# Moving one set of small matmuls ahead of another in a fused attention and MLP kernel

## The chip, the cores and the metric

The kernel runs on one core of a Trainium2 chip. The metric is the device time of one execution in microseconds. Three runs of the kernel before gave 688.54, 688.73 and 689.0 us, a median of 688.73 us. Beside these there is one profiled execution, with its own time and its own trace; all durations below come from it.

The core's engines work side by side, each through its own queue: TensorE does matmuls (PE in the profile; its weight loads are PEld), VectorE (DVE) and ScalarE (ACT) do the elementwise work, and SyncE (SP) issues the transfers. An instruction that needs another engine's result waits for it on a semaphore.

## The reference

There are 8 batches of 8 heads, 512 tokens, 32 state rows and a head width of 64. For each batch and head, the tokens read the state and the state reads the tokens, both through a softmax:

```
xread = softmax(scale * x @ state^T) @ state      # 512 rows a head
sread = softmax(scale * state @ x^T) @ x          # 32 rows a head
attn  = concat([xread, sread])                    # 544 rows a batch
h     = attn_as_4352_by_512 @ w_in                # w_in: 512 x 2048
out   = (h * sigmoid(1.702 h)) @ w_out            # w_out: 2048 x 512
```

The weights come as float64 values. The kernel reads them as pairs of 32-bit words and makes float32 values of them on the chip.

## The kernel before, in words

**Weights.** Each weight matrix is brought in as 16 pieces, the 16 of `w_in` first. A piece of `w_out` is a transfer of 512 KB into a buffer named `later` (`load_weight`, line 199), and then a series of steps called a round. On VectorE: a mask of the exponent bits (line 221), the fraction (239), the sign (245) and two products (258 and 264). On ScalarE, between the mask and the sign: two Relu instructions (lines 232 and 233, in `round_a`) that clamp the exponent to the range of float32. This document calls the pair the clamp. `powers_to` and `round_to` issue these steps ahead of need, so one call of `round_to` finishes one piece and starts the clamp of the next.

**The state, multiplied early.** The kernel doesn't compute `xread @ w_in` as it stands. `att_M(b, c)` (line 575) multiplies the state of batch b by column block c of `w_in` and keeps the product in a tile M; `up_x` (line 671) then multiplies M by the transposed attention weights (`aT`) in one step. `att_M` issues 16 small matmuls (64 rows by 32 columns of the array, line 430) into two PSUM banks, and two ScalarE copies (line 573) bring these into M. With its third argument set, the two banks are the pair with the tag `h`, which `up_x` also uses.

**The state's own read.** `att_sread(b)` (line 618) issues 64 small matmuls (128 by 32, line 629) and two ScalarE copies (line 635). For batch 1 it reads `eT`, which two VectorE transposes (line 605, `eT_turn`) make from a tile that has come back from HBM. `att_srT` (line 638) transposes the result on TensorE.

**Where the change lies.** The order of the work is that of the Python text: nothing is planned by costs, each engine takes its instructions in the order written. From line 1562 a loop over 8 block pairs computes batch 0's `gelu(h) @ w_out` by one step of Strassen's method: seven products P1 to P7 a pair, each of four matmuls (`pair`, line 1548), with sums of blocks made on VectorE by `pair_sums` and `left_sums` (line 1479). In between it completes `h` of batch 1 with `up_x`. The first pass (i = 0, lines 1568 to 1589) also holds the attention work that was left over: `att_sread(0)`, `att_M(1, 2)`, the transposes of `eT`, a `round_to`, `att_sread(1)` and `att_M(1, 3, True)`. After it, from line 1665 on, each batch goes through `strassen_two`, where a product has a second level of Strassen's method (lines 809 and 858) and the next batch's attention is hung into named places.

At line 1574 only one piece, number 19, is left for `round_to(nin + 4, 1)` to finish, and what it issues on ScalarE is the clamp of piece 20, whose mask (line 221) waits for that piece's transfer. Line 1583 is `up_x(1, 8)`. Its output takes the next bank of the pair `h`, which is the first of the two that `att_M(1, 3, True)` has just filled, so it can't begin before the first of that call's copies.

Of the kernel before, what the change touches and what calls it, by code (L numbers as in the profile page):

```python
# [20 lines left out]
def kernel(  # L21
# [72 lines left out]
    def att_ps(shape, name):  # L94
        return psA.tile(shape, FP32, tag="att", name=name)
# [151 lines left out]
    def round_b(i, ahead, follows, fill=None):  # L247


        if i not in begun:  # L250
            fraction(i)
        if i not in signed:
            sign(i)
        dst, sc = begun.pop(i), signed.pop(i)
        lo, _ = words(i)
        powers_to(ahead)

        nc.vector.scalar_tensor_tensor(dst, lo, 2.0**-32, dst.bitcast(I32), ALU.mult, ALU.add)
        del raw[i]
        if fill is not None:  # L260
            fill()
        elif follows and i + 1 in raw:
            fraction(i + 1)
        nc.vector.scalar_tensor_tensor(dst, dst, 2.0**-20, sc.bitcast(FP32), ALU.mult, ALU.mult)
# [13 lines left out]
    def powers_to(n):  # L278
        while done["a"] < min(n, len(PIECES)):
            load_weights(done["a"] + 1)  # L280
            round_a(done["a"])
            done["a"] += 1

    def refill():
        while done["b"] > NPR and done["load"] < len(PIECES) and before(done["load"]) < done["b"]:
            load_weights(done["load"] + 1)

    def round_to(n, ahead=AHEAD):

        nin = NFC * NPR  # L290
        while done["b"] < min(n, len(PIECES)):
            i = done["b"]
            powers_to(i + 1)
            round_b(i, min(i + 1 + ahead, i + 3 if i > nin + 3 else i + 2 if i >= nin else nin), i >= nin or i + 1 < nin and (i + 1 < n or i >= NPR))
            done["b"] += 1
            refill()
# [128 lines left out]
    def by_state(b, ps, rhs):  # L425

        for j in range(NPR):
            for g in range(NG):
                rows, st = slice(D * g, D * (g + 1)), slice(Ns * j, Ns * (j + 1))
                nc.tensor.matmul(ps[g][st], state_of(b, NG * j + g, g), rhs(rows, j), start=True, stop=True)  # L430
# [140 lines left out]
    def M_copies(b, c):  # L571
        for g, ps in enumerate(M_banks.pop((b, c))):
            nc.scalar.copy(A[b]["M", c][:, g], ps)  # L573

    def att_M(b, c, spare=False, banks=None, copied=True):

        m = mpool.tile([P, NG, FC], FP32, tag=f"M{turns['M'] % NFC if b < 2 else c}", name=f"M_{b}_{c}")
        turns["M"] += 1
        A[b]["M", c] = m
        name = f"M_{b}_{c}_"  # L580
        ps = banks or [
            psH.tile([P, FC], FP32, tag="h", name=name + str(g)) if spare else att_ps([P, FC], name + str(g)) for g in range(NG)
        ]
        by_state(b, ps, lambda rows, j: w_in[c][rows, j])
        M_banks[b, c] = ps
        if copied:
            M_copies(b, c)
# [15 lines left out]
    def eT_turn(b, g):  # L603
        t = A[b]["eT"][:, g].rearrange("p c q -> p (c q)")
        nc.vector.transpose(t, t)
# [12 lines left out]
    def att_sread(b):  # L618

        a = A[b]  # L620
        ps = att_ps([P, NG, D], f"sr_{b}")
        for g in range(NG):
            for c in range(SCH):
                for j in range(NPR):
                    st = slice(Ns * j, Ns * (j + 1))
                    e, v = a["eT"][:, g, c, st], xn[b][:, NG * j + g, c]
                    if b:
                        e = a["eT"][:, g, j, Ns * c : Ns * (c + 1)]
                    nc.tensor.matmul(
                        ps[st, g], e, v,  # L630
                        start=(c == 0), stop=(c == SCH - 1),
                    )
        sr = apool.tile([P, P], FP32, tag="sr", name=f"sr_{b}", bufs=2)
        for g in range(NG):
            nc.scalar.activation(out=sr[:, D * g : D * (g + 1)], in_=ps[:, g], func=AF.Copy, scale=a["e2"][g][1])
        A[b]["sr"] = sr
# [11 lines left out]
    def gelus(n):  # L648
        for _ in range(n):
            fn, kw = waiting.pop(0)  # L650
            fn(**kw)
# [19 lines left out]
    def up_x(b, f, spare=False, bank=None, wait=False, dst=None):  # L671
        c, o = divmod(P * f, FC)
        m = A[b]["M", c]
        up(b, f, S, [m[:, g, o : o + P] for g in range(NG)], [A[b]["aT"][:, g] for g in range(NG)], spare, bank, wait, dst)
# [796 lines left out]
    def pieces(t, *shape):  # L1471
        n, k = shape
        return t.rearrange("p a b -> p (a b)").rearrange("p (n k t) -> p n k t", n=n, k=k)
# [7 lines left out]
    def four(t):  # L1481
        return t.rearrange("p a b -> p (a b)").rearrange("p (n t) -> p n t", t=HS)
# [15 lines left out]
    def turns_of(*lists):  # L1498

        for step in zip(*lists):  # L1500
            for fn, args in step:
                fn(*args)
# [4 lines left out]
    def left_sums(i):  # L1507

        u = ORDER[i] // 2
        (a11, a21), (a12, a22) = quarters(0, u, S), quarters(0, HF // 2 + u, S)  # L1510
        s1, s2, *s4 = (v[:, i % 4 : i % 4 + 2] for v in s_rooms)
        return [(tt, v) for v in ((s1, a21, a22, ALU.add), (s2, s1, a11), (a21, a11, a21), *((s, a12, s2) for s in s4))]
# [18 lines left out]
    def pair(i, *names):  # L1531

        f = ORDER[i]
        a11, a12, a21, a22 = a_of(f)
        s1, s2, s4 = s_of(i) if i >= 0 and names[0] not in ("P1", "P2") else (None,) * 3
        t = t24(i) if s1 is not None else None
        for name in names:
            lhs, rhs = {
                "P1": lambda: (a11, B11[:, f]),
                "P2": lambda: (a12, B21[:, f]),  # L1540
                "P5": lambda: (s1, T1[:, f]),
                "P6": lambda: (s2, t[:, 0]),
                "P7": lambda: (a21, B12[:, f]),
                "P3": lambda: (s4, B22[:, f]),
                "P4": lambda: (a22, t[:, 1]),
            }[name]()
            for r in range(2):
                nc.tensor.matmul(  # L1548
                    ps7[name][:, HN * r : HN * (r + 1)], lhs[:, P * r : P * (r + 1)], rhs,
                    start=(i == 0 and r == 0), stop=(i == HF - 1), skip_group_check=True,  # L1550
                )
# [10 lines left out]
    for i in range(HF):  # L1562
        round_to(nin + 2 * i + 2)
        gelus(len(waiting))
        if i == 3:
            nc.scalar.copy(G[1, f_early // 2][:, f_early % 2], early)
        if i == 0:
            pair(i, "P1")
            att_sread(0)
            att_M(1, 2, banks=bank_o[1::2])  # L1570
            turns_of(left_sums(0))
            for g in range(NG):
                eT_turn(1, g)
            round_to(nin + 4, 1)
            att_sread(1)
            att_M(1, 3, True)
            t_room.append(pieces(apool.tile([P, NG, SCH * P], FP32, tag="eT", name="t_room_1"), 2, 2))
            s_rooms.append(four(apool.tile([P, NG, NB * Ns], FP32, tag="e1", name="s4_room")))
            pair_sums(i, left_sums(0)[3:])
            pair(i, "P2")  # L1580
            f_early = rest.pop(0)
            early = xn[0].rearrange("p h c d -> p (h c d)")[:, :S]
            up_x(1, f_early, dst=early)
            att_srT(0)
            att_srT(1)
            powers_to(nin + 6)
            pair(i, "P6")
            ps7["P7"], ps7["P3"] = (psH.tile([P, FC], FP32, tag="h", name=f"down_{k}") for k in (7, 3))
            ps7["P4"], up_bank = (att_ps([P, FC], f"down_{k}") for k in (4, "up"))
        else:  # L1590
            pair_sums(i)
            pair(i, "P1", "P2")
        if i == 2:
            G[1, f_early // 2] = free.pop(0)
        if i > 1 and i % 2 == 0:
            up_x(1, rest.pop(0), bank=up_bank, wait=True)
        if i == HF - 1:
            k1 = s_rooms[0][:, :2]
            nc.scalar.copy(k1, ps7["P1"].rearrange("p (r n) -> p r n", r=2))
        late()  # L1600
        if i > 1 and i % 2:
            up_x(1, rest.pop(0), bank=up_bank if i < HF - 1 else bank_o[0], wait=True)
        if i == HF // 2 + 1:
            load_state(2)
            load_x_squares(2)
# [140 lines left out]
```

## Time and profile before

| what | value |
|---|---|
| median of three runs | 688.73 us |
| the profiled execution's own time | 689.52 us |
| its span, first to last instruction | 687.7 us |
| TensorE busy (matmuls) | 677.1 us, 98% |
| VectorE busy | 558.6 us, 81% |
| ScalarE busy | 327.4 us, 48% |
| mean granted TensorE clock | 0.998 |

The span and the profiled time differ by 1.8 us, which lie around the instructions. A difference in the span is taken as a difference in the time. In the answers below, a line of the timeline reads: start in us from the span's beginning, length in us, engine, source line, operation, what it writes and reads, tile of the array for matmuls, elements, count; a last bracket gives idle time of that engine before it, and what ended it. The line is often that of a helper. A matmul's end is modelled, and the next one normally starts before it, so the distance between two starts says better than a length what a group costs in a full stream.

### The profile page before, as it was taken

The page shows a single profiled execution, that of the slowest core. Times are in us where ns is not written, and L with a number is a line of the kernel's source. Part 1 is how long each engine was busy: PE and PEld are TensorE (multiplying, and loading weights), DVE is VectorE, ACT ScalarE, POOL GpSimd, SP SyncE. Part 2 cuts the span into 40 slices and gives each one's busy share as a digit, 9 for nine tenths or more (in the row PEclk, how much of TensorE's full clock was granted, in tenths as well). Part 3 has the DMA queues.
Part 4 walks back from the last instruction along what each step waited for, and adds up shares of the span by engine and source line. Part 5 has one row for each costly group of instructions (what it writes and reads, how often), then busy time and mean ns, then how long its engine had stood idle before and what let it go on. Part 6 is the DMA issues. An engine that isn't in the chain of part 4 may idle for free.

```text
span 687.7 us, 13606 instructions
## 1 busy us (share of the span) xinstructions
PE 677.1 (98%) x5347; PEld 577.8 (84%) x5347; DVE 558.6 (81%) x1066; ACT 327.4 (48%) x725; POOL 1.5 (0%) x10
## 2 busy tenths in 40 slices
PE   8999999999999999999999999999999999999996
PEld 4443587769989899889988998989988998999995
DVE  5999999999999886888878796888688885986540
ACT  7799844124355543752365435553375237421410
POOL 0000000000000000000000000000000000000000
PEclk9999999999999999999999999999999999999999
DMA  9731545338262764256443755176415640251000
GB/s 317 303 102 32 174 152 139 112 112 274 91 139 95 200 188 122 34 150 204 142 78 104 208 151 112 32 203 188 121 31 161 194 150 5 77 167 48 2 2 30
DMA packets 101391, 88.44 MB, mean 129 GB/s; under 512 B 56656, under 2 KB 80720, under 8 KB 101328
## 3 DMA queue, kind: packets, MB, share of 16 engines
q1 hardware_dynamic: 100784, 87.45, 43.2%
q8 instruction: 42, 0.69, 0.4%
q10 hardware_dynamic: 544, 0.13, 0.1%
q14 instruction: 21, 0.17, 0.1%
HBM read 69.47 MB, written 18.09 MB: 127 GB/s over the span
## 4 chain that ended last, share of the span: by engine, by line
PE 89%; DVE 5%; DMA 3%; ACT 2%; issue 0%; DVEq 0%; ACTq 0%
PE low L809 28%; PE o L1219 15%; PE o L809 15%; PE upx L1219 6%; PE o L1548 4%; PE M L430 3%; PE down L1548 3%; PE o L708 3%; PE upw L1219 2%; PE o L858 2%; PE down_up L662 1%; PE h L662 1%; PE o L430 1%; PE upx_sr L1219 1%; DMA out_dram<-osb_sr 1%; DVE low L245 1%
## 5 line engine op out<-in xcount | busy, mean ns | idle before, releaser
L809 PE MATMUL low<-w_out,g_room 128*128 128x128 f32 x416 | 54.3, 276 | 0.0
L809 PEld LDWEIGHTS low<-w_out,g_room 128*128 128x128 f32 x416 | 50.5, 192 | 4.5 <-issue 4.2
L1219 PE MATMUL o<-ta,M 128*128 128x256 f32 x192 | 49.9, 382 | 0.0
L1219 PE MATMUL upx<-aT,M 128*128 128x256 f32 x192 | 49.3, 379 | 0.0
L809 PE MATMUL low<-low,g_room 128*128 128x128 f32 x336 | 43.3, 275 | 0.0
L1219 PEld LDWEIGHTS o<-ta,M 128*128 128x128 f32 x192 | 35.5, 190 | 5.9 <-ACT g_room L1265 1.6
L809 PEld LDWEIGHTS low<-low,g_room 128*128 128x128 f32 x336 | 40.3, 192 | 0.0
L1219 PEld LDWEIGHTS upx<-aT,M 128*128 128x128 f32 x192 | 36.0, 190 | 4.7
L1225 ACT ACTIVATE g_room<-o 128x512 f32<-128x512 f32 (+1 forms) x56 | 31.3, 559 | 10.4 <-PE o L1219 10.4
L809 PE MATMUL low<-sums,later 128*128 128x128 f32 x272 | 34.9, 275 | 0.0
L573 ACT COPY M<-M 128x512 f32<-128x512 f32 x53 | 27.5, 596 | 14.7 <-PE M L430 14.7
L809 PEld LDWEIGHTS low<-sums,later 128*128 128x128 f32 x272 | 32.7, 192 | 0.1
L865 DVE TENSOR_TENSOR g_room<-g_room 128x512 f32<-128x512 f32 x48 | 31.8, 686 | 0.2
L232 ACT ACTIVATE low<-low,edge 128x512 f32<-128x512 int32 x31 | 22.5, 727 | 17.4 <-DVE low L221 17.4
L1219 PE MATMUL o<-ta,ms 128*128 128x256 f32 x120 | 30.8, 379 | 0.0
L1265 ACT COPY g_room<-o 128x512 f32<-128x512 f32 (+1 forms) x28 | 15.5, 555 | 25.4 <-PE o L1219 25.4
L1225 ACT ACTIVATE g_room<-g_room 128x512 f32<-128x512 f32 (+1 forms) x28 | 16.8, 600 | 20.8 <-DVE g_room L1228 20.8
L1219 PEld LDWEIGHTS o<-ta,ms 128*128 128x128 f32 x120 | 22.8, 190 | 3.1
L1219 PE MATMUL o<-aT,m 128*128 128x256 f32 x96 | 24.6, 379 | 0.0
L809 PEld LDWEIGHTS o<-w_out,g_room 128*128 128x128 f32 x160 | 19.4, 192 | 5.0 <-issue 5.0
L430 PE MATMUL M<-w_in,stT 64*32 64x512 f32 x344 | 23.2, 592 | 0.0
L233 ACT ACTIVATE low<-low,edge 128x512 int32<-128x512 f32 x31 | 22.4, 722 | 1.1
(321 smaller groups left out, 1637.9 us busy)
## 6 DMA issues: line engine op xcount, KB each, us to landing
low<-low SPq DMA_DIRECT2D x108, 256.0 KB, 2.6
low<-low SPq DMA_DIRECT2D x11, 768.0 KB, 5.8
later<-in_moe_w_out_dram SPq DMA_DIRECT2D x16, 512.0 KB, 3.5
w_out<-in_moe_w_in_dram SPq DMA_DIRECT2D x12, 512.0 KB, 4.4
xsq<-in_x_dram SPq DMA_DIRECT2D x96, 64.0 KB, 2.3
xn<-in_x_dram SPq DMA_DIRECT2D x12, 512.0 KB, 4.4
out_dram<-osb SPq DMA_DIRECT2D x15, 256.0 KB, 2.2
squares<-e SPq DMA_DIRECT2D x28, 128.0 KB, 2.5
```

The source lines that it names most:

```text
L232: nc.scalar.activation(out=sc.bitcast(FP32), in_=sc, func=AF.Relu, bias=edge[0], scale=-8.0)
L233: nc.scalar.activation(out=sc, in_=sc.bitcast(FP32), func=AF.Relu, bias=edge[1], scale=-1.0)
L430: nc.tensor.matmul(ps[g][st], state_of(b, NG * j + g, g), rhs(rows, j), start=True, stop=True)
L573: nc.scalar.copy(A[b]["M", c][:, g], ps)
L662: nc.tensor.matmul(hps, lhs[i], rhs[i], start=(i == 0), stop=(i == n - 1))
L708: nc.tensor.matmul(ps[:, r], lhs[f][:, P * r : P * (r + 1)], rhs[:, f], start=(first and r == 0 and f == 0), stop=(f == HF - 1), skip_grou ...
L809: nc.tensor.matmul(ps, lhs[f], rhs[:, f], start=(first and f == 0), stop=(f == QF - 1), skip_group_check=True)
L865: nc.vector.tensor_tensor(out=out, in0=x0, in1=x1, op=op)
L1219: nc.tensor.matmul(ps[:, k], lhs[i][:, o : o + P], rhs[i], start=(first and k == 0 and i == 0), stop=(i == n - 1), skip_group_check=True,)
L1225: nc.scalar.activation(out=dst, in_=src, func=AF.Gelu_apprx_sigmoid)
L1265: nc.scalar.copy(c12, Y(u))
L1548: nc.tensor.matmul(ps7[name][:, HN * r : HN * (r + 1)], lhs[:, P * r : P * (r + 1)], rhs, start=(i == 0 and r == 0), stop=(i == HF - 1), s ...
```

## The change

One call moves up two lines. `att_M(1, 3, True)` is issued before `round_to(nin + 4, 1)` and `att_sread(1)`, no longer after them. No instruction is added or removed.

```diff
             turns_of(left_sums(0))
             for g in range(NG):
                 eT_turn(1, g)
+            att_M(1, 3, True)
             round_to(nin + 4, 1)
             att_sread(1)
-            att_M(1, 3, True)
             t_room.append(pieces(apool.tile([P, NG, SCH * P], FP32, tag="eT", name="t_room_1"), 2, 2))
             s_rooms.append(four(apool.tile([P, NG, NB * Ns], FP32, tag="e1", name="s4_room")))
             pair_sums(i, left_sums(0)[3:])
```

On TensorE the 16 matmuls of the last M now stand right behind those of `att_M(1, 2)`, and the 64 of `att_sread(1)` behind both. On ScalarE the two copies of that M now stand ahead of the clamp of piece 20 and ahead of the two copies of `att_sread(1)`. The queues of VectorE and SyncE hold the same instructions in the same order as before; `att_M` issues neither VectorE work nor a transfer.

## The prediction

> **What bounds the kernel now.** I read the page first. Its line of busy times says that TensorE bounds the kernel:
>
> ```profile
> PE 677.1 (98%) x5347; PEld 577.8 (84%) x5347; DVE 558.6 (81%) x1066; ACT 327.4 (48%) x725; POOL 1.5 (0%) x10
> ```
>
> So 10.6 us of the 687.7 us span are idle on TensorE, and only a change that removes such idle time, or adds some, moves the end. The waits of TensorE in the whole run show just two near the change (0.8 and 0.3 us), and none after 83 us: from there on TensorE is never recorded idle. The timeline of TensorE from 68 to 90 us shows both:
>
> ```profile
> 73.94 1.10 PE L629 MATMUL sr<-xn,eT 128*32 128x64 f32 x64
> 74.97 1.09 PE L430 MATMUL o<-w_in,two 64*32 64x512 f32 x16
> 76.39 1.20 PE L629 MATMUL sr<-sums,eT 128*32 128x64 f32 x64 [0.33 <-DVE eT L605]
> 77.52 1.09 PE L430 MATMUL M<-w_in,two 64*32 64x512 f32 x16
> 78.54 1.13 PE L1548 MATMUL o<-w_out,sums 128*128 128x256 f32 x4
> 80.50 1.98 PE L662 MATMUL h<-low,M 128*128 128x512 f32 x4 [0.83 <-ACT M L573]
> 82.32 0.38 PE L640 MATMUL srT<-ident,sr 128*128 128x128 f32 x2
> 82.54 1.03 PE L1548 MATMUL o<-t_room,s_room 128*128 128x256 f32 x4
> ```
>
> In order: read 0, M of column block 2, a wait for the transposed eT, read 1, M of block 3, P2, a wait for a copy of that M, `up_x(1, 8)`, the two srT, P6. ScalarE's timeline and the chain tell why that copy is late:
>
> ```profile
> 76.15 1.07 ACT L573 COPY M<-o 128x512 f32<-128x512 f32 x2 [0.28 <-PE o L430]
> 78.08 0.72 ACT L232 ACTIVATE low<-low,edge 128x512 f32<-128x512 int32 x1 [0.86 <-DVE low L221]
> 78.84 0.72 ACT L233 ACTIVATE low<-low,edge 128x512 int32<-128x512 f32 x1
> 79.47 0.50 ACT L635 ACTIVATE sr<-sr,sm 128x64 f32<-128x64 f32 x2
> 79.86 1.07 ACT L573 COPY M<-M 128x512 f32<-128x512 f32 x2
> ```
>
> ```profile
> 71.53 6.07 DMA later<-in_moe_w_out_dram
> 78.08 0.73 ACT low L232
> 79.97 0.48 ACT M L573
> 80.50 1.98 PE h L662 x4
> ```
>
> The transfer of piece 20 lands at 77.60, its mask ends at 78.05, the clamp follows, and the copies of M queue behind the clamp and the read's copies, though M itself was there at about 78.6. The waiting `up_x` needs only the bank. The chain runs from the transfer through ScalarE into TensorE.
>
> **What the Trainium skill says.** "PSUM — Partial Sum Buffer", section "Engine vs sequencer instructions", states that ScalarE's queue is strictly first in, first out and that matmuls start in program order; the trace agrees, as M's copy waits from 78.6 to 79.86 behind two instructions that it doesn't use. "TensorE: Matmul & The Clock Gate", section "Single matmul latency", gives a constant of about 166 ns beside the streaming of a matmul, so a wait costs more than the gap between modelled ends; P2's four start 0.86 us before the next group in a full stream (82.54 to 83.40), so the wait cost 80.50 - 78.54 - 0.86 = 1.10 us, not 0.83. Its Part 1 says that idleness can lower the clock; the granted clock is 1.00 in each 2 us stretch from 72 to 82 us, so nothing is to be had there.
>
> **The change part by part.** It adds no instruction and moves 16 matmuls and 2 copies; no mask, transfer or VectorE step changes its place. The sum is made on starts, from 74.97 to the start of `up_x`.
>
> Before: 80.50 - 74.97 = 5.53 us. After, if nothing waits, TensorE does two M, read 1 and P2. Two M back to back are shown in a later batch, with the start of what follows:
>
> ```profile
> 152.62 1.92 PE L430 MATMUL M<-w_in,stT 64*32 64x512 f32 x32
> 154.48 3.72 PE L858 MATMUL o<-w_out,g_room 128*128 128x256 f32 x16
> ```
>
> That is 1.86 us (1.88 where it follows a read, 178.17 to 180.05). Read 0 took 74.97 - 73.94 = 1.03; read 1 is the same shape, and its 1.13 before holds a little waiting for the second transpose. P2 is 0.86. Sum: 1.88 + 1.03 + 0.86 = 3.77 us, against 5.53: a gain of 1.76 us. No run shows a read followed by a product of full tiles; changing from M to P2 cost up to 0.14 more than the rate of M in pairs (1.02 against 0.93 to 0.88), so I allow 0.0 to 0.14 and take 0.06. **Gain 1.70 us**; `up_x` starts at 78.80.
>
> Each wait has to be checked against that:
> - M of block 3 starts at about 75.9. Its two `h` banks were last read by copies (L616) that end at 74.1, and its tile by `up_x` on batch 1's second column block, long over. Cover 1.8 us.
> - Read 1 would start at 76.85. The first transpose ends at 76.25 and both by 76.87 (1.30 for two from 75.57); the second half of the read starts 0.5 later. The 0.33 us wait goes, hidden by the moved M; without that cover it would stay.
> - The copies of M: the first two copies hold ScalarE from 76.15 to 77.11 at their pitch of 0.48, the moved ones follow from 77.11 to 78.2. The bank is free at 77.7, 1.1 us before `up_x`. Clamp: its mask is there at 78.05, so it starts some 0.05 to 0.15 later than 78.08. Behind it are the read's copies (to 80.1 at most, not 79.97), for which the second srT waits at 80.8, and later VectorE's sign of piece 20, which runs only at 83.50: 3.7 us of cover after the clamp's end at 79.8.
> - VectorE is busy without a break from 77.6 to 151.5, so none of its results comes earlier. What TensorE reads of them meets it 1.7 us sooner. P6, at 82.54 before, then wants its sum at 80.84, P7 at 82.57 and P3 at 83.43. VectorE's lines:
>
> ```profile
> 79.96 0.42 DVE L1479 TENSOR_TENSOR t_room<-w_out,sums 128x256 f32<-128x256 f32 x1
> 80.30 0.68 DVE L1479 TENSOR_TENSOR s_room<-sums,s_room 128x512 f32<-128x512 f32 x1
> 81.24 0.42 DVE L1479 TENSOR_TENSOR w_out<-w_out 128x256 f32<-128x256 f32 x1
> 153.08 1.31 DVE L455 STREAM_TRANSPOSE e<-o 128x512 f32<-128x512 f32 x2 [1.54 <-PE o L430]
> ```
>
> P6's sum is done at 80.38 (cover 0.46, the thinnest), P7's at 81.66 (0.9), P3's at 80.98. The 80.30 step writes where read 1 read; that read now ends about 0.3 us later, at 78.0: cover 2.3. In the pairs after it each product has 2.7 us or more left: the second piece of pair 3 is done at 97.25 and its P2 starts at 101.52, 99.8 after. At 144.63 the next batch's state is turned into a bank that VectorE frees at 141.9: cover 1.0 of 2.7 is left. At 151.5 VectorE runs out of work and waits 1.54 us for TensorE; it then moves along by about 1.6 us, and its next wait for TensorE (0.23 us, at 158.29) takes the rest.
> - SyncE: its transfers wait for VectorE in this stretch, and stay where they are. From 151 us everything follows TensorE.
>
> Span: 687.7 - 1.7 = 686.0. The profiled execution's own time is 689.52, 0.79 above the median of 688.73; a difference carries over, so the time is 688.73 - 1.7 = **687.03 us**.
>
> **The rivals.**
> 1. A later wait takes part of it. VectorE doesn't move for 74 us, and TensorE comes 1.7 us sooner: if signalling eats the 0.46 us before P6, or one of the other covers was read too large, TensorE waits again. For it: VectorE is 99% busy from 90 to 141 us (50.6 of 51). Against it: the smallest cover is still positive. If half of the gain goes, 687.9; it falls under 0.2% once TensorE loses 0.3 us of it.
> 2. It does nothing: all of the lead is lost where TensorE meets a transfer or VectorE before 151.5 us (no such wait is recorded), or `up_x` still waits for something besides the bank. 688.7. For it: the wait named is the last one only.
> 3. Slower: TensorE's queue now holds read 1, P2 and all else behind the moved M. If M's banks or tile came free only with a ScalarE step after the first M's copies, the wait would move to M. Its break-even start is 75.9 + 1.7 = 77.6. Were it the clamp's end at 79.6, `up_x` would start at 79.6 + 1.02 + 1.03 + 0.86 = 82.5, 2.0 us late: 690.7. Against it: the last readers end at 74.1, 3.5 us before break-even.
>
> **How the numbers follow.** Runs of this kernel lie within 0.5 us, so about 0.2% (1.38 us) can be told from no change. The full gain of 1.6 to 1.8 gets 0.68, the partial one 0.16, nothing 0.09, slower 0.07. The likeliest case alone spans 686.7 to 687.4 with a median's scatter of 0.2 to 0.3. The range takes in most of the partial case: 686.6 to 688.0 us. Faster by over 0.2% (below 687.35): 0.68, the first case with a scatter that gives and takes alike; within 0.2%: 0.25, the partial and the empty case; slower: 0.07.
>
> **What would show it.** Right: M of block 3 runs straight after that of block 2 from about 75.9 as a group of 32; read 1 has no bracket; `up_x` starts near 78.8 without the bracket of 0.83; P6 near 80.9; the clamp stands behind four copies and starts by 78.3; VectorE's waits at 151.5 us are gone or under 0.1. Wrong: a new bracket on TensorE between 75.9 and 85, a VectorE step ahead of it; P1 of batch 1 (141.18 before) less than 1.5 us earlier; or the lead there at 141 and gone by 200.

## The result, and the profile after

The changed kernel takes 687.87 us (median of 22 runs, 687.43 to 688.44) against 688.77 us for the kernel before in 22 runs beside them. The ratio is 0.9984, with a 95% interval of 0.9977 to 0.999: faster, by 0.9 us between the medians and by 1.1 us (0.7 to 1.6) by the ratio. The forecast of 687.03 us was 0.84 too low; the measured time lies in the forecast range, near its upper end.

The page of the profiled execution after (its own time 687.92, its span 686.1 us) has this line of busy times:

```profile
PE 676.9 (99%) x5347; PEld 578.0 (84%) x5347; DVE 558.4 (81%) x1066; ACT 328.0 (48%) x725; POOL 1.5 (0%) x10
```

The span is 1.6 us shorter and TensorE's work is the same, so the difference is idle time of TensorE. The timeline of TensorE around the change, to be set beside that of before:

```profile
73.60 1.10 PE L629 MATMUL sr<-xn,eT 128*32 128x64 f32 x64
74.63 1.09 PE L430 MATMUL o<-w_in,two 64*32 64x512 f32 x16
75.51 1.06 PE L430 MATMUL M<-w_in,two 64*32 64x512 f32 x16
76.64 1.25 PE L629 MATMUL sr<-sums,eT 128*32 128x64 f32 x64
77.82 1.13 PE L1548 MATMUL o<-w_out,sums 128*128 128x256 f32 x4
78.78 1.88 PE L662 MATMUL h<-low,M 128*128 128x512 f32 x4
80.50 0.38 PE L640 MATMUL srT<-ident,sr 128*128 128x128 f32 x2
80.81 1.13 PE L1548 MATMUL o<-t_room,s_room 128*128 128x256 f32 x4
```

Both brackets are gone. The two M run back to back, read 1 follows, and `up_x(1, 8)` starts 0.96 us after P2, where it started 1.96 after it before. ScalarE's timeline shows why, and VectorE's shows what is late now:

```profile
75.81 1.07 ACT L573 COPY M<-o 128x512 f32<-128x512 f32 x2 [0.28 <-PE o L430]
76.77 1.09 ACT L573 COPY M<-M 128x512 f32<-128x512 f32 x2
78.45 0.72 ACT L232 ACTIVATE low<-low,edge 128x512 f32<-128x512 int32 x1 [0.58 <-DVE low L221]
79.83 0.50 ACT L635 ACTIVATE sr<-sr,sm 128x64 f32<-128x64 f32 x2
```

```profile
75.87 1.31 DVE L605 STREAM_TRANSPOSE eT<-eT 128x512 f32<-128x512 f32 x2 [1.52 <-DMA eT<-squares]
80.33 0.42 DVE L1479 TENSOR_TENSOR t_room<-w_out,sums 128x256 f32<-128x256 f32 x1
```

The copies of M stand ahead of the clamp and are over 0.9 us before `up_x` needs the bank. In this execution eT came late, so VectorE waited 1.52 us for it; read 1 lost 0.28 us in all and P6 waited for its sum, which ended at 80.75.

One measure is used from here on: the stretch from the start of read 0 to the start of P5 of pair 0. It was 83.40 - 73.94 = 9.46 us before and is 81.78 - 73.60 = 8.18 us after, so 1.28 of the 1.6 us between the spans lie there. The other 0.34 were there already when read 0 began (73.94 against 73.60), ahead of the change: the first transfers of the kernel landed sooner (the matmuls that wait for the state start at 6.79 us, against 7.15). From P5 to the end nothing is lost or gained: P1 of batch 1 starts 1.62 us earlier (141.18 and 139.56).

So the trace says 1.28 us for the stretch, and the timed runs say 0.9 to 1.1. The forecast said 1.70. The experiments ask where that went.

### The profile page after: what moved, and what is told of

It reads as the page before. It is cut to its first block, busy times and chain, and to the rows that moved or that the text cites. A ratio compares the mean times of both kernels' runs of the same rounds, so it can differ in the third digit from the quotient of the medians.

```text
span 686.1 us, 13606 instructions
## 1 busy us (share of the span) xinstructions
PE 676.9 (99%) x5347; PEld 578.0 (84%) x5347; DVE 558.4 (81%) x1066; ACT 328.0 (48%) x725; POOL 1.5 (0%) x10
## 4 chain that ended last, share of the span: by engine, by line
PE 89%; DMA 4%; ACT 3%; DVE 3%; SPq 0%; issue 0%; DVEq 0%; ACTq 0%
PE low L809 28%; PE o L1219 15%; PE o L809 15%; PE upx L1219 6%; PE o L1548 4%; PE M L430 3%; PE down L1548 3%; PE o L708 3%; PE upw L1219 2%; PE o L858 2%; PE down_up L662 2%; PE h L662 1%; PE sr L629 1%; PE o L430 1%; PE upx_sr L1219 1%; ACT low L233 1%
```

## The experiments

### Both kernels again

> The kernel before, once more, for a second profile of the stretch from the start of read 0 to the start of P5 of pair 0 (9.46 us in the first profile of before, 8.18 in that of after, so 1.28 of the 1.6 us between the spans; the other 0.3 us lie at the start of the kernel, ahead of the change). Theory A, the gain is a fixed property of the queues: the stretch is 9.4 to 9.5 us again and the wait of up_x on the copy 0.8 us. Theory B, the first profile had late transfers and the loss follows the landing of piece 20: with an earlier landing the stretch is 8.8 to 9.2 us, and the clamp starts sooner after read 0 than 4.14 us.

> The changed kernel once more. Theory A: the stretch from read 0 to P5 is 8.1 to 8.3 us again, 1.3 below before, and the time about 0.9 to 1.3 us below before. Theory B: the stretch moves by some tenths with the landing of the tile that eT is made from (3.3 to 4.0 us after the start of read 0 it can be read).

Measured: before, 688.95 us (14 runs; ratio to the 54 runs beside them 1.0, 0.9992 to 1.0008). After, 687.88 us (17 runs; 0.9983, 0.9976 to 0.999). The second profile of before has a stretch of 8.78 us, 0.68 less than the first, and it isn't the same stretch made shorter. TensorE's timeline:

```profile
75.04 1.09 PE L430 MATMUL o<-w_in,two 64*32 64x512 f32 x16
76.06 0.80 PE L629 MATMUL sr<-sums,eT 128*32 128x64 f32 x41
77.54 0.54 PE L629 MATMUL sr<-sums,eT 128*32 128x64 f32 x23 [0.68 <-issue]
78.01 1.09 PE L430 MATMUL M<-w_in,two 64*32 64x512 f32 x16
79.03 1.13 PE L1548 MATMUL o<-w_out,sums 128*128 128x256 f32 x4
79.99 1.88 PE L662 MATMUL h<-low,M 128*128 128x512 f32 x4
```

Here `up_x` doesn't wait at all: it starts 0.96 us after P2. Read 1 begins on time and then stops after 41 of its 64 matmuls, for 0.68 us, waiting for nothing that the profile shows ("issue"). VectorE and ScalarE, in the same profile:

```profile
74.68 1.30 DVE L605 STREAM_TRANSPOSE eT<-eT 128x512 f32<-128x512 f32 x2
```

```profile
77.18 0.74 ACT L232 ACTIVATE low<-low,edge 128x512 f32<-128x512 int32 x1
79.19 1.07 ACT L573 COPY M<-M 128x512 f32<-128x512 f32 x2
```

eT came 0.9 us earlier than in the first profile, the clamp ran 0.9 us earlier, and the copies wait for M, no longer for the clamp. Theory A falls. Theory B has the size about right and the cause only in part, for it knows of no stop inside the read. The after kernel's second profile has the shortest stretch of the two, 7.71 us, with no wait in it:

```profile
75.96 1.06 PE L430 MATMUL M<-w_in,two 64*32 64x512 f32 x16
76.95 1.10 PE L629 MATMUL sr<-sums,eT 128*32 128x64 f32 x64
77.98 1.13 PE L1548 MATMUL o<-w_out,sums 128*128 128x256 f32 x4
78.95 1.88 PE L662 MATMUL h<-low,M 128*128 128x512 f32 x4
```

### Half of the change, and another bank

```diff
 # copy_first: copies ahead of the clamp, matmuls in the order of before
-            round_to(nin + 4, 1)
             att_sread(1)
             att_M(1, 3, True)
+            round_to(nin + 4, 1)
```

> Half of the change: the order on TensorE stays as before (read 1, then M), but the copies of M stand ahead of the clamp, behind the read's copies. If the clamp in front of the copies is what costs: the wait of up_x for the copy is gone, the wait of read 1 for the transpose (0.3 us or more) stays, the stretch from read 0 to P5 is 8.3 to 8.5 us and the time 0.7 to 1.1 us below before. If it is the place of the matmuls that counts: the stretch stays near 9.4 us and the time is that of before.

```diff
 # other_bank: all orders of before
-            up_x(1, f_early, dst=early)
+            up_x(1, f_early, bank=bank_o[3], dst=early)
```

> The order of before everywhere, but up_x(1, 8) writes to the bank of P5, which is free since the copies of the first M, and no longer to that of the last M. If only the bank holds up_x: it starts right behind P2 though the copies are as late as before, the stretch is 8.3 to 8.5 us and the time 0.7 to 1.1 us below before, as for the copies moved alone. If up_x waits for something else of ScalarE's: the stretch stays near 9.4 us.

Measured: copies first 688.61 us (14 runs; 0.9993, 0.9985 to 1.0001), other bank 688.54 us (22 runs; 0.9992, 0.9986 to 0.9999), each beside 688.87 of before. Both traces show `up_x` right behind P2 (0.97 us). With copies first it starts ahead of the clamp (79.45 against 79.60 us), so it doesn't wait for that. The trace of the other bank settles less: there the first copy of the last M, begun at 80.02, would have been over ahead of `up_x` at 80.83 in any case, so that the bank is what held it rests on the timed runs. The gain is 0.3 us between the medians (0.5 and 0.6 by the ratio), below what was expected, and the interval of copies first includes 1. The profile of the other bank has the longest stretch of all, 9.52 us, and this line says where:

```profile
78.37 0.54 PE L629 MATMUL sr<-sums,eT 128*32 128x64 f32 x23 [1.41 <-issue]
```

Again the read stops after 41 matmuls, now for 1.41 us. So the wait for the clamp is not the only loss, and in this execution it is none.

### What the read waits for

A stop at the same matmul in two kernels, with no semaphore behind it, suggests that TensorE has no instructions. The page of before has a queue for that:

```profile
q8 instruction: 42, 0.69, 0.4%
```

Its 42 packets are 16 KB each. TensorE's 2 x 5347 matmuls and weight loads make 41.8 blocks of 256, so the queue is TensorE's. The Trainium skill, "Runtime: NRT & Kernel Launch", section "Instruction fetch mechanics", says that each engine's instructions are streamed in blocks of 16 KiB (256 instructions) by its own transfers, and that this is mostly hidden; the count agrees, and whether the fetch is hidden is the question here. Asked microsecond by microsecond, the transfer view has one such packet in the six us ahead of each read 1. From 71 to 72 us in the first profile of before, and from 75 to 76 in the second (packets, MB, share of 16 engines):

```profile
q8 instruction: 1, 0.02, 6.5%
```

```profile
q8 instruction: 1, 0.02, 5.7%
```

Narrower windows put the starts at 71.1 and 75.1. The packet occupies one of the 16 transfer engines for 1.04 us (6.5% of 16) and 0.91 us. So there are two courses: either the block comes ahead of eT, and eT is late; or it comes behind eT and in the midst of the weights, eT is early, and read 1 outruns its instructions (so far an inference from the times). Which it is hangs on little: in the first profile SyncE issues eT's transfer from 71.10 to 71.44 us and that of the next piece of weights from 71.53 on, and the packet starts at 71.13. The 128 instructions of a read take 1.03 us, so a block lasts 2.1 us at that rate; the 8 instructions of a product of a pair take 0.86.

The next kernel moves these blocks. Twenty more matmuls at the start put every later instruction 40 further on in the stream:

```diff
 # before_shift; after_shift is the same edit in the changed kernel
-    keep_warm(14)
+    warm = psH.tile([P, FC], FP32, tag="h", name="warm")
+    for n in [FC] * 10 + [16] * 24:
+        nc.tensor.matmul(warm[:, :n], zeros[:, :P], zeros[:, :n], start=True, stop=True)
```

> The kernel before with 20 more matmuls at its start: of the 14 warming matmuls, which compute nothing that is used, 4 give way to 24 with 16 columns. So each instruction of TensorE comes 40 later in its stream, and the 16 KB transfers of the queue of TensorE's instructions fall 40 instructions earlier in the work. Theory C, fetching: in usual runs of before read 1 stops for 0.7 to 1.4 us because TensorE's next instructions come late, their transfer queued behind those of eT and of the weights; with the shift that transfer is over before eT's begins, read 1 runs through, the stretch from read 0 to P5 is 7.8 to 8.1 us, against 8.8 in the second profile of before, and the time is 0.7 to 1.0 us below before although the order of before is kept. Theory A, the clamp in front of the copies: the stretch stays at 8.8 to 9.5 and the time is that of before.

> The changed kernel with the same 20 more matmuls at its start. Theory C: it has no stop to lose, so the stretch is 7.7 to 7.8 us and the time 0.8 to 1.1 us below before; it differs from before with the shift by 0.3 us at most, which is what the change is worth without the stop. Theory A: it lies about 1 us below before with the shift.

Measured: before with the shift 688.44 us (13 runs; 0.9993, 0.9984 to 1.0001), after with it 687.73 us (20 runs; 0.9981, 0.9974 to 0.9988), beside 689.06 of before. The block is now there at 61.6 us. TensorE has started 337 matmuls by then, of 5367; in the first profile of before it had started 339, of 5347, when the block came at 71.1. So the block is tied to a place in TensorE's stream and not to a time (in the second course it comes some 80 matmuls after that place, behind eT's transfer), and the shifted kernel has 43 such packets, not 42. From that place to the stop, after the 41st matmul of read 1, are 135 matmuls, 270 instructions: about one block. TensorE in the shifted kernel before:

```profile
75.93 1.10 PE L629 MATMUL sr<-sums,eT 128*32 128x64 f32 x64
76.96 1.09 PE L430 MATMUL M<-w_in,two 64*32 64x512 f32 x16
77.98 1.13 PE L1550 MATMUL o<-w_out,sums 128*128 128x256 f32 x4
79.47 1.98 PE L662 MATMUL h<-low,M 128*128 128x512 f32 x4 [0.36 <-ACT M L573]
```

The stop is gone and read 1 starts on time, since eT is early too. That much of theory C holds: the stop comes with the place of the blocks, so the fetch is not hidden here. (One profile without a stop proves little; the count over all profiles is below.) But the stretch is 8.50 us, not 7.8 to 8.1: with the read on time, P2 ends sooner, and `up_x` waits for the copies again. Theory C alone is half of the cause. The changed kernel with the shift has a stretch of 7.70, as expected; by the ratio the shift gives it about 0.2 us (0.9981, against 0.9984 and 0.9983 without it), within the intervals. It lies 0.7 us below the shifted kernel before, not 0.3.

### The other half, and a further step

```diff
 # late_copies: the matmuls of the change, the copies where they were
+            att_M(1, 3, True, copied=False)
             round_to(nin + 4, 1)
             att_sread(1)
-            att_M(1, 3, True)
+            M_copies(1, 3)
```

> The other half of the change: the matmuls of the last M stand ahead of read 1, as in the change, but its copies stay behind the clamp and the read's copies. Theory C: the stop in read 1 is gone, as M takes longer an instruction than the read and gives the transfer of instructions 0.65 us more; what is left is the wait for the copies, small where the weights come early, so the stretch is 7.8 to 8.2 us and the time 0.5 to 0.9 us below before. Theory A: the copies decide, the stretch is 8.8 to 9.5 us and the time that of before.

```diff
 # p2_first, on the changed kernel
             att_M(1, 3, True)
+            pair(i, "P2")
             round_to(nin + 4, 1)
             att_sread(1)
 ...
             pair_sums(i, left_sums(0)[3:])
-            pair(i, "P2")
```

> The changed kernel with P2 of pair 0 moved up as well, between the last M and read 1, since it needs neither. Read 1 then starts 0.86 us later and finds its transposes and its instructions there in every run. Against the changed kernel: nothing where read 1 doesn't wait (a stretch of 7.7 us), 0.2 to 0.4 us less where it does (as in the first profile of after, 8.18 us). So 0.9 to 1.2 us below before, and 0.0 to 0.2 below the changed kernel in the median. If the later end of read 1 held up VectorE's next sum, the stretch would be longer, 8.0 us or more.

Measured: late copies 688.72 us (13 runs; 0.9994, 0.9986 to 1.0002), P2 first 687.85 us (18 runs; 0.9984, 0.9977 to 0.9991), beside 689.06. With late copies the read runs through, 64 matmuls from 76.87, although the block of instructions came at 74.9; but `up_x` waits, and the stretch is 8.94 us, not the 7.8 to 8.2 expected:

```profile
79.99 1.98 PE L662 MATMUL h<-low,M 128*128 128x512 f32 x4 [0.96 <-ACT M L573]
```

So moving the matmuls did away with the stop, and moving the copies does away with the wait, and each alone only makes room for the other. The first has little to spare: read 1 now meets the end of the block after 25 matmuls, at about 77.27 us (an estimate from its 1.03 us for 64), and the packet ended at 75.84, 1.4 us sooner; in the four executions with a stop TensorE went on 1.4 to 1.5 us after the end of the packet. A block that comes later could still stop it; no run shows that. With P2 ahead of the read nothing waits either, but the stretch is 7.91 us, 0.20 longer than the shortest of the change: P2 takes 1.06 us ahead of the read, and `up_x` behind the read 1.83, against 0.97 and 1.72. The median is that of the change.

### Both waits away, without the change

> Both waits taken away with the matmuls left in their order of before: the 20 more matmuls at the start move the transfers of TensorE's instructions, and the copies of the last M stand ahead of the clamp. Theory D, two waits that cover each other: each of the two alone gave a third to a half of the gain, as the other wait then shows; together they give nearly all of it, a stretch from read 0 to P5 of 7.8 to 7.95 us and a time 0.8 to 1.1 us below before, like the change. If the back-to-back M of the change saves something of its own beyond 0.15 us: the stretch stays above 8.1 us.

This kernel has the shift of the start and the order of `copy_first`; the last M stays behind read 1. Measured: 687.82 us (21 runs; 0.9984, 0.9977 to 0.999), beside 688.95. TensorE:

```profile
76.08 1.10 PE L629 MATMUL sr<-sums,eT 128*32 128x64 f32 x64
77.11 1.09 PE L430 MATMUL M<-w_in,two 64*32 64x512 f32 x16
78.13 1.13 PE L1550 MATMUL o<-w_out,sums 128*128 128x256 f32 x4
79.10 1.88 PE L662 MATMUL h<-low,M 128*128 128x512 f32 x4
```

A stretch of 7.87 us and the ratio of the change, by two edits that each gave 0.07% alone, with intervals that include 1. This is what theory D expects: two waits that cover each other. What the back-to-back M save of their own is small, 0.16 us between the 7.87 here and the 7.71 of the change.

### How often before takes which course

> The kernel before, a third profile, to see which of its two courses it takes. If the 16 KB transfer of TensorE's instructions starts near 71 us, eT is transposed from about 75.5 on, read 1 runs late but whole, up_x waits 0.8 us for the copy, and the stretch is 9.3 to 9.5 us; if it starts near 75, eT is transposed from about 74.7 on, read 1 stops after 41 of 64 matmuls for 0.6 us or more, up_x waits less than 0.3 us, and the stretch is 8.7 to 9.5 us by the length of the stop.

> The kernel before, a fourth profile, with the same two courses: instructions near 71 us with eT late and the wait on the copy, or near 75 us with eT early and the stop in read 1.

> The kernel before, a fifth profile, with the same two courses. If the median of before belongs to the second course, at least two of these three show it, with own times of 688.6 to 689.0 us.

All executions that were profiled, in us. "Read 1" is what was lost before and within read 1 against 1.03 us at the rate of a full stream, "`up_x`" its start less that of the group ahead of it and 0.97, the distance where it doesn't wait (1.03 where the read stands ahead of it):

| kernel | block of instructions at | eT transposed from | read 1 | `up_x` | stretch | own time |
|---|---|---|---|---|---|---|
| before, first | 71.1 | 75.57 | 0.50 | 0.99 | 9.46 | 689.52 |
| before, fourth | 71.1 | 75.58 | 0.50 | 0.73 | 9.21 | 689.28 |
| before, second | 75.1 | 74.68 | 0.92 | 0 | 8.78 | 688.90 |
| before, third | 74.9 | 74.49 | 0.70 | 0 | 8.57 | 688.52 |
| before, fifth | 75.0 | 74.39 | 1.11 | 0.12 | 9.21 | 689.00 |
| after, first | 70.8 | 75.87 | 0.28 | 0 | 8.18 | 687.92 |
| after, second | 74.6 | 74.71 | 0 | 0 | 7.71 | 687.88 |
| copies first | 71.1 | 75.52 | 0.43 | 0 | 8.30 | 688.24 |
| other bank | 75.1 | 74.78 | 1.65 | 0 | 9.52 | 689.69 |
| late copies | 74.9 | 74.64 | 0 | 1.12 | 8.94 | 689.04 |
| P2 first | 75.1 | 74.51 | 0 | 0 | 7.91 | 687.85 |
| before, shifted | 61.6 | 74.55 | 0 | 0.52 | 8.50 | 688.45 |
| after, shifted | 62.2 | 75.03 | 0 | 0 | 7.70 | 688.27 |
| shifted, copies first | 61.7 | 74.72 | 0 | 0 | 7.87 | 688.02 |

Three of the five executions of before take the second course, with stops of 0.68, 0.45 and 0.87 us. The third profile's own time, 688.52, lies below the 688.6 to 689.0 that was expected of that course. Where the block comes near 71 us, eT is transposed from 75.5 or later, in four of four; where it comes elsewhere, from 75.03 or sooner, in ten of ten. Of the nine profiles with read 1 ahead of the last M, the four with the block near 75 us have the stop, and the five with it at 71.1 or before have none. That the block's packet itself is what holds up eT, and what decides which of the two goes first, was not tried.

## Why the prediction was right or wrong

**The queues.** Right. The copies stood behind the clamp, `up_x` waited for the first of them (it starts 0.63 or 0.64 us after that copy's start in each of the five profiles in which it waits), and with the change the clamp stands behind four copies and starts up to 0.7 us after its mask (78.17 against 77.47 in the second profile of after), at no cost. One reading was short: from 78.6 to 79.86 the copy of M stood behind four instructions, the clamp's two and the read's two copies, not behind two.

**The new stretch.** Right, to a tenth, where eT is early. In the second profile of after, two M take 1.88 us, read 1 takes 1.03, and `up_x` starts 3.88 us after the first M, where the prediction had 3.77 + 0.06. P2 was mis-sized: it takes 0.97 ahead of `up_x`, not 0.86. The stretch of 9.46 less the gain of 1.70 is 7.76; it measured 7.71 with eT early and 8.18 with eT late.

**The covers.** Right from P5 on: TensorE waits for nothing from there to the end, and the lead of 1.62 us at P1 of batch 1 is there at the end. VectorE's waits for TensorE between 83 and 160 us are gone in the first profile of after, as forecast; in the second, where eT was early, 0.47 and 0.23 us of them are left. The cover of 2.7 us or more in the later pairs is 2.6 by the prediction's own figures (97.25 and 99.8). The thinnest cover, 0.46 us ahead of P6, didn't hold in the first profile of after: there eT came 0.64 us later against read 0 than in the profile that the cover was read from, and P6 and P5 lost about 0.2 us together.

**The size of what is removed: this term was mis-sized.** The prediction took the wait of the one profiled execution and wrote that "a difference carries over", so that the 0.79 us between that execution's own time and the median stayed out of the sum. It doesn't carry over. In the five executions of before the own time less the stretch is 679.8 to 680.1 us, so nearly all of what sets them apart lies in the stretch, in the very waits that the change removes. The execution that the prediction read has the longest of the five, 9.46 us; the second, with an own time close to the median, has 8.78. The mean of the five is 9.05, that of the two of after is 7.95, and the difference of 1.10 us is what the timed runs show (1.1 by the ratio). So of the 0.6 us that are missing from the 1.70, 0.4 were never there to be removed in an average execution of before, and 0.2 are lost again after the change when eT is late, where the prediction let nothing wait.

The first profile belongs to one of two courses, and in the other, which three of five executions took, the loss in this place is another: not the transpose and the clamp, but the read's own instructions, which the prediction didn't know of. The gain of the moved matmuls comes from those: read 1 meets the end of the block about 0.6 us later (an estimate: two M of 1.88 us and 25 matmuls of the read now stand ahead of it, where one M of 1.02 and 41 matmuls stood).

**The rivals.** The first happened only in small, in the 0.2 us at P6 and P5 of one profile. It ends at 687.9 us, which is the measured time, but by another way: less was there to be gained. So it is luck that the room left for it took in the measured time; the likeliest case, 686.7 to 687.4 us, did not. The chance of 0.68 for a gain above 0.2% was too high: the measured 0.16% (0.10 to 0.23) is mostly below it.

## What to carry to other kernels

A profile shows one execution; where its own time lies above the median, ask first whether the excess lies in the wait that a change is to remove, for then it must not be counted. Two waits in a row can hide each other, so undoing one tells little of the other: before saying that a wait is worth nothing, remove both. And in this kernel a run of small matmuls uses up TensorE's instructions some 13 times as fast as a product of full tiles (128 in 1.03 us, against 8 in 0.86): where a stop shows in such a run while large transfers are under way, try putting slower instructions ahead of it.

## What was not expected of the hardware

TensorE stopped in the midst of a group of 64 small matmuls with no semaphore to wait for, for 0.45, 0.68, 0.87 and 1.41 us in four executions, each time after the 41st. Each time it went on 1.4 to 1.5 us after the end of the 16 KB packet of its instruction queue (76.0 to 77.54, 75.75 to 77.12, 75.9 to 77.43, and 77.0 to 78.37, where the packet itself took 1.84 us, not 0.9). A shift of 40 instructions at the start of the kernel, 70 us earlier, put that packet at 61.6 or 61.7 us and removed the stop, in both shifted kernels that keep read 1 ahead of the last M. That the packet is what TensorE waited for is inferred from these times; the profile names no cause for the stop.
